# The tail rows of two batches stored by one transfer instead of two, and the last stores issued by SyncE alone

## Chip, cores and metric

One core of one Trainium2 chip runs the kernel. The metric is the device time of one execution in microseconds (us), lower is better. Three executions of the kernel before took 319.03, 319.62 and 318.98 us; the median is 319.03 us.

## The reference

A linear attention feeds a gated feed-forward layer. B = 8 batches of 576 tokens, 8 heads of 64 columns, so 4608 tokens of width 512; the hidden width is 1536. All is float32 at the borders.

```python
kv  = einsum('bhsd,bhse->bhde', k, v)
att = einsum('bhsd,bhde->bhse', q, kv)
att = att / sqrt(mean(att * att, -1) + 1e-6) * g_norm
x   = att.transpose(0, 2, 1, 3).reshape(4608, 512)
xn  = x / sqrt(mean(x * x, -1) + 1e-6) * rms_g
out = (silu(xn @ w_gate) * (xn @ w_val)) @ w_out      # (4608, 512) float32
```

## The kernel before

**Tokens.** Each batch has 576 tokens. The kernel takes the first 512 (`MAIN`) of each batch as one block, blocks 0 to 7. The last 64 (`TAIL`) of all eight batches make a ninth block, number 8, again 512 tokens. Block 8 is cut into four chunks of 128 tokens; chunk `c` holds the tail of batch `2c` in partitions 0 to 63 and that of batch `2c + 1` in partitions 64 to 127. In the output these two groups of 64 rows are each contiguous (64 rows of 2 KB), but they lie 576 rows apart.

**Stages of a block.** Class `Att` makes the normalised rows of a block. Class `Ffn` multiplies them: `up(j)` for the 12 slices of the hidden width (gate and value products of TensorE into two PSUM banks, SiLU on ScalarE, product on VectorE), then four times a down product of 128 tokens (12 matmuls into one PSUM bank), a copy of that bank to SBUF, and a store. The order is written out by hand: the loop over `n` runs `up` for 12 units and then a down product for 4 units, with the attention work of the next block hung between the units. In block 8 nothing is hung in any more.

**The down products of the last block.** For chunks 0, 1 and 2 of block 8, `down` runs 12 matmuls of 512 columns (L529), `down_out` copies the bank on ScalarE (L104, called from L537) and stores it from SyncE (L542). For chunk 3, `down_last` splits the 512 output columns into three parts of 256, 128 and 128 columns in three PSUM banks (L567). Two of them are copied by ScalarE (L104) and the last by VectorE (L106); the columns 0 to 255 are stored after the first copy, and the columns 256 to 511 after the third (L576).

**The buffers of the stores.** The tile `o_sb` is 128 partitions by two chunks by 512 columns of float32, and its pool has two buffers that are taken in turn. Chunks 0 and 1 of block 8 share one buffer, chunk 2 has the other, and `down_last` takes a new tile, which is the buffer of chunks 0 and 1 again. So the first copy of chunk 3 waits until the stores of chunks 0 and 1 have landed.

**Queues.** All loads and stores are issued by SyncE (queue q1 of the profile) but for three small groups issued by ScalarE (queue q10): two loads of `v` at the start, the two norm vectors (`gam`, L601 and L602), and one store of chunk 3. The program ends (L1069) when SyncE has seen the last store land.

Of the kernel before, what the change touches and what calls it, by code (L numbers as in the profile page):

```python
# [20 lines left out]
def kernel(  # L21
# [12 lines left out]
    nc = tc.nc  # L34

    B, H, S, D = q.shape
    d_model = H * D
# [5 lines left out]
    MAIN = 128 * T  # L43
    TAIL = S - MAIN
# [57 lines left out]
    def cast(engine, dst, src):  # L102
        if engine is SC:
            engine.copy(out=dst, in_=src)  # L104
        else:
            engine.tensor_copy(out=dst, in_=src)  # L106
# [161 lines left out]
    class Att:  # L268
        def __init__(self, n):
            self.n = n  # L270
            self.tail = n == B
            self.outa = {}
            self.xna = {}
            self.sq = {}
            self.qt = None
# [186 lines left out]

    class Ffn:
        def __init__(self, n):
            self.n = n
# [66 lines left out]
        def down_out(self, c, engine=None):  # L534
            if c % 2 == 0:
                self.o_sb = osb_pool.tile([128, 2, d_model], FP32, name="o_sb")
            cast(engine or SC, self.o_sb[:, c % 2, :], self.o_ps[c])  # L537
            n = self.n
            if n == B:
                for u in range(2):  # L540
                    r0 = (2 * c + u) * S + MAIN
                    nc.sync.dma_start(  # L542
                        out=out[r0 : r0 + TAIL, :], in_=self.o_sb[u * TAIL : (u + 1) * TAIL, c % 2, :]
                    )
            elif c % 2 == 1 and n == 0:
                r0 = 256 * (c // 2)
                rows = out[r0 : r0 + 256, :].rearrange("(p c t) d -> t p c d", c=2, t=2)
                for t in range(2):
                    nc.sync.dma_start(out=rows[t], in_=self.o_sb[64 * t : 64 * t + 64])
            elif c % 2 == 1:  # L550
                rows = out[n * S : n * S + MAIN, :].rearrange("(p t) d -> p t d", t=T)[:, c - 1 : c + 1, :]
                nc.sync.dma_start(out=rows, in_=self.o_sb)
# [5 lines left out]
        def down_last(self, c):  # L558

            o_sb = osb_pool.tile([128, 2, d_model], FP32, name="o_sb")[:, 0, :]  # L560
            parts = (
                (0, 256, ops_pool, "o_ps", SC), (256, 384, gps_pool, "g_ps", SC), (384, 512, vps_pool, "v_ps", DVE),
            )
            for lo, hi, p, nm, engine in parts:
                ps = p.tile([128, MAIN], FP32, name=nm)[:, 0 : hi - lo]
                for j in range(NF):
                    PE.matmul(  # L567
                        ps, lhsT=self.h[:, j, c * 128 : (c + 1) * 128], rhs=wo_sb[:, j, lo:hi],
                        start=(j == 0), stop=(j == NF - 1),
                    )  # L570
                cast(engine, o_sb[:, lo:hi], ps)
                for d0, done in ((0, 256), (256, 512)):
                    if hi == done:
                        for u in range(2):
                            r0 = (2 * c + u) * S + MAIN
                            (nc.sync if u or hi < d_model else nc.scalar).dma_start(  # L576
                                out=out[r0 : r0 + TAIL, d0:done], in_=o_sb[u * TAIL : (u + 1) * TAIL, d0:done]
                            )

# [15 lines left out]
    for j in (0, 1):  # L597
# [5 lines left out]
        out=gam[NS : NS + 1, :].rearrange("o (i d) -> o i d", i=2),  # L603
        in_=g_norm.rearrange("(o d) -> o d", o=1).unsqueeze(1).to_broadcast([1, 2, D]),
# [97 lines left out]
    for j in (0, 1):  # L702
# [29 lines left out]
        out=gsq, in0=gcol, scalar=1.0 / d_model, in1=gcol, op0=OP.mult, op1=OP.mult  # L732
# [257 lines left out]
    for n in range(1, B + 1):  # L990
# [12 lines left out]
        if n < B:  # L1003
# [5 lines left out]
            for i in range(2):  # L1009
                u = o0 + 2 * i  # L1010
# [9 lines left out]
        b = n + 2  # L1020
# [53 lines left out]
```

## Time and profile before

| | |
|---|---|
| median of three executions | 319.03 us |
| the profiled execution, its own time | 319.61 us |
| its span, first to last instruction | 317.6 us |
| mean granted TensorE clock | 0.998 |
| busy: TensorE matmul / VectorE / ScalarE | 308.5 / 181.3 / 175.6 us |
| stores of chunks 0 to 2 of block 8 (L542) | 6, of 128 KB each |
| stores of chunk 3 (L576) | 4, of 64 KB each |

The profiled execution took 319.61 us, of which 317.6 us lie between its first and last instruction and 2.0 us around them. Three other executions have their median 0.58 us below it. A busy TensorE says that matmuls were in flight, not that it ran at its peak. A busy share is a mean over the whole run: the change concerns the last 12 us alone, and what those wait for has to be read from that stretch.

### The profile page before, as it was taken

What the parts mean: (1) busy time and instruction counts of PE and PEld (TensorE: products, weight loads), DVE (VectorE), ACT (ScalarE), POOL (GpSimd) and SP (SyncE); (2) the same over time, 40 slices, a digit from 0 to 9 for tenths busy, and PEclk for the clock granted to TensorE, in tenths of its full rate; (3) what the DMA queues carried; (4) which work ended last, traced back from release to release, by engine and by line L of the source; (5) the groups of instructions that cost most, each with busy time, mean ns of one, the idle gap of its engine ahead of it and who ended that gap; (6) DMA issues with size and microseconds to landing.
All of it is one profiled execution on the core that took longest, in us unless ns stands there. A gap on an engine that the chain in (4) does not pass through costs nothing.

```text
span 317.6 us, 5996 instructions
## 1 busy us (share of the span) xinstructions
PE 308.5 (97%) x2334; PEld 150.3 (47%) x2371; DVE 181.3 (57%) x378; ACT 175.6 (55%) x323; POOL 21.5 (7%) x46
## 2 busy tenths in 40 slices
PE   7899999999999999999999999999999999999995
PEld 3575446444444444444444444444444444444443
DVE  3776768679339922893289327941795079504310
ACT  3577367485667465746683768376745374233321
POOL 1174351100000000000000000000000000000000
PEclk9999999999999999999999999999999999999999
DMA  7999999685369267904790489939002710230014
GB/s 266 358 385 388 375 375 333 145 275 215 90 180 344 86 138 187 369 9 108 189 378 22 98 172 207 354 66 181 22 0 60 140 66 3 57 141 3 0 33 100
DMA packets 60712, 54.95 MB, mean 173 GB/s; under 512 B 36232, under 2 KB 45708, under 8 KB 60684
## 3 DMA queue, kind: packets, MB, share of 16 engines
q1 hardware_dynamic: 60304, 53.92, 56.7%
q10 hardware_dynamic: 380, 0.66, 0.6%
q8 instruction: 18, 0.29, 0.4%
q14 instruction: 10, 0.08, 0.1%
HBM read 37.75 MB, written 9.44 MB: 149 GB/s over the span
## 4 chain that ended last, share of the span: by engine, by line
PE 90%; DMA 5%; SPq 1%; another core or an unknown queue 1%; issue 1%; POOL 1%; DVE 0%; ACT 0%
PE v_ps L477 28%; PE g_ps L477 28%; PE o_ps L529 26%; DMA st<-in_moe_w_val_dram 3%; DMA st<-in_q_dram 2%; PE att_ps L286 2%; PE v_ps L529 1%; PE g_ps L529 1%; DMA out_dram<-o_sb 1%; PE att_ps L326 1%; PE o_ps L494 1%; POOL wv_sb L191 1%; PE o_ps L326 0%; PE att_ps L262 0%
## 5 line engine op out<-in xcount | busy, mean ns | idle before, releaser
L483 DVE TENSOR_TENSOR h_sb<-silu,v_ps 128x512 bf16<-128x512 bf16 x104 | 71.1, 684 | 99.9 <-ACT silu L482 68.1
L477 PE MATMUL v_ps<-xnt,wv_sb 128*128 128x512 bf16 x409 | 106.2, 379 | 0.7
L477 PE MATMUL g_ps<-xnt,wg_sb 128*128 128x512 bf16 x398 | 104.6, 379 | 0.7
L482 ACT ACTIVATE silu<-g_ps 128x512 bf16<-128x512 f32 x104 | 62.1, 597 | 70.1 <-PE g_ps L477 58.4
L529 PE MATMUL o_ps<-wo_sb,h_sb 128*128 128x512 bf16 x386 | 86.8, 379 | 0.4
L477 PEld LDWEIGHTS <-wv_sb 128*128 128x128 bf16 x416 | 40.7, 98 | 49.1
L529 PEld LDWEIGHTS <-h_sb 128*128 128x128 bf16 x420 | 40.6, 98 | 47.6 <-issue 0.4
L477 PEld LDWEIGHTS <-wg_sb 128*128 128x128 bf16 x416 | 39.5, 98 | 46.4
L104 ACT COPY o_sb<-o_ps 128x512 f32<-128x512 f32 (+1 forms) x34 | 19.6, 581 | 40.2 <-PE o_ps L529 36.6
L373 DVE TENSOR_TENSOR xna<-outa,s1y 128x512 bf16<-128x512 bf16 x28 | 17.9, 685 | 0.0
L104 ACT CAST qb<-st 128x512 bf16<-128x512 f32 (+1 forms) x30 | 16.2, 603 | 3.0 <-DMA st<-in_q_dram 3.0
L104 ACT CAST vb<-st 128x576 bf16<-128x576 f32 x25 | 15.7, 673 | 3.4 <-DMA st<-in_v_dram 3.4
L356 DVE TENSOR_REDUCE ssq<-sq 128x16 f32<-128x1024 bf16 x14 | 17.1, 1220 | 0.5
L356 DVE TENSOR_REDUCE ssq<-sqt 128x16 f32<-128x1024 bf16 x14 | 17.1, 1220 | 0.5
L104 ACT CAST kb<-st 128x576 bf16<-128x576 f32 x20 | 12.5, 673 | 0.0
L341 ACT ACTIVATE sq<-att_ps 128x512 bf16<-128x512 f32 x14 | 7.6, 594 | 4.3 <-PE att_ps L326 3.6
L355 DVE TENSOR_TENSOR sq<-sq,gsq 128x512 bf16<-128x512 bf16 x14 | 5.9, 422 | 4.9 <-ACT sq L341 4.9
L629 PE MATMUL att_ps<-kv_all 128*128 128x512 bf16 (+1 forms) x21 | 7.5, 486 | 1.2 <-DVE sel L618 1.2
L106 DVE CAST kb<-st 128x576 bf16<-128x576 f32 x12 | 6.1, 527 | 3.6 <-DMA st<-in_k_dram 3.5
L106 POOL CAST wo_sb<-st 128x512 bf16<-128x512 f32 x12 | 7.3, 635 | 7.4 <-DMA st<-in_moe_w_out_dram 7.4
L341 ACT ACTIVATE sqt<-o_ps 128x512 bf16<-128x512 f32 x14 | 7.6, 597 | 0.0
L347 ACT CAST outa<-o_ps 128x512 bf16<-128x512 f32 x14 | 7.5, 591 | 0.0
(150 smaller groups left out, 181.5 us busy)
## 6 DMA issues: line engine op xcount, KB each, us to landing
st<-in_k_dram SPq DMA_DIRECT2D x7, 1152.0 KB, 10.5
st<-in_v_dram SPq DMA_DIRECT2D x7, 1152.0 KB, 12.6
out_dram<-o_sb SPq DMA_DIRECT2D x14, 512.0 KB, 3.1
st<-in_q_dram SPq DMA_DIRECT2D x6, 1024.0 KB, 7.2
st<-in_moe_w_out_dram SPq DMA_DIRECT2D x6, 512.0 KB, 10.4
st<-in_moe_w_gate_dram SPq DMA_DIRECT2D x4, 512.0 KB, 10.4
st<-in_moe_w_val_dram SPq DMA_DIRECT2D x4, 512.0 KB, 9.8
st<-in_k_dram SPq DMA_DIRECT2D x4, 288.0 KB, 4.0
```

The costliest lines, as they stand in the source:

```text
L104: engine.copy(out=dst, in_=src)
L106: engine.tensor_copy(out=dst, in_=src)
L286: PE.matmul(self.kv_ps[x][to, a, :], lhsT=kb[rows, 2 * a + x, c, :], rhs=vb[rows, 2 * a + x, c, :], start=(a == 0 and c == 0), stop=(a == ...
L341: SC.activation(out=self.in_place(self.sq[i][:, 0], g), in_=bank, func=ACT.Square)
L347: SC.copy(out=self.in_place(rows, g), in_=bank)
L356: DVE.reduce_sum(out=self.ssq[:, c], in_=sq, axis=AX.X)
L373: DVE.tensor_tensor(out=self.xna[c], in0=self.outa[c], in1=self.alpha[:, c, :].to_broadcast([128, H, D]), op=OP.mult)
L477: PE.matmul(ps, lhsT=wt[:, s, j * 128 : (j + 1) * 128], rhs=x[:, s, :], start=(s == 0), stop=(s == NS - 1),)
L482: SC.activation(out=silu, in_=g_ps, func=ACT.Silu)
L483: DVE.tensor_tensor(out=self.h[:, j, :], in0=silu, in1=v_ps, op=OP.mult)
L529: PE.matmul(self.o_ps[c], lhsT=self.h[:, j, c * 128 : (c + 1) * 128], rhs=wo_sb[:, j, :], start=(j == 0), stop=(j == NF - 1),)
L629: PE.matmul(ps[:, 0:w], lhsT=warm_sb[:, 0:128], rhs=warm_sb[:, 0:w], start=True, stop=True, skip_group_check=True)
```

## The change

The two stores of a chunk of block 8 (partitions 0 to 63 to one batch's rows, partitions 64 to 127 to the next batch's) become one. Its SBUF side is all 128 partitions; its DRAM side is a view of the output with three dimensions, 2 batches by 64 rows by 512 columns, the batches 576 rows apart. The stores of chunk 3 become two transfers of 2 by 64 by 256, both issued by SyncE, where one of the four was issued by ScalarE before. Ten transfers become five; the bytes are the same. No other instruction is added, removed or moved.

```diff
+    tail_rows = out.rearrange("(b s) d -> b s d", s=S)[:, MAIN:S, :]
...
         def down_out(self, c, engine=None):
...
             if n == B:
-                for u in range(2):
-                    r0 = (2 * c + u) * S + MAIN
-                    nc.sync.dma_start(
-                        out=out[r0 : r0 + TAIL, :], in_=self.o_sb[u * TAIL : (u + 1) * TAIL, c % 2, :]
-                    )
+                nc.sync.dma_start(out=tail_rows[2 * c : 2 * c + 2], in_=self.o_sb[:, c % 2, :])
...
         def down_last(self, c):
...
                 for d0, done in ((0, 256), (256, 512)):
                     if hi == done:
-                        for u in range(2):
-                            r0 = (2 * c + u) * S + MAIN
-                            (nc.sync if u or hi < d_model else nc.scalar).dma_start(
-                                out=out[r0 : r0 + TAIL, d0:done], in_=o_sb[u * TAIL : (u + 1) * TAIL, d0:done]
-                            )
+                        nc.sync.dma_start(out=tail_rows[2 * c : 2 * c + 2, :, d0:done], in_=o_sb[:, d0:done])
```

## The prediction

> **What bounds the kernel now.** I read the page first: span and engines, DMA queues, then the end of the chain, the instructions of the end, and single stretches of DMA.
>
> ```profile
> span 317.6 us, 5996 instructions
> PE 308.5 (97%) x2334; PEld 150.3 (47%) x2371; DVE 181.3 (57%) x378; ACT 175.6 (55%) x323; POOL 21.5 (7%) x46
> DMA packets 60712, 54.95 MB, mean 173 GB/s; under 512 B 36232, under 2 KB 45708, under 8 KB 60684
> q1 hardware_dynamic: 60304, 53.92, 56.7%
> q10 hardware_dynamic: 380, 0.66, 0.6%
> ```
>
> TensorE is busy throughout, so up to 313.8 us the kernel is bound by matmuls, and the change leaves those alone. What it touches is the end. The chain of waits there, and the timeline of the same stretch (start, duration, what):
>
> ```profile
> 311.22 0.59 ACT o_sb L104
> 311.82 0.02 issue
> 311.83 2.11 DMA out_dram<-o_sb
> 313.95 0.28 DVE o_sb L106
> ```
>
> ```profile
> 306.65 6.29 SPq L542 DMA_DIRECT2D out_dram<-o_sb  x6
> 312.58 0.37 ACT L104 COPY o_sb<-o_ps 128x256 f32<-128x256 f32 x1 [0.77 <-PE o_ps L567]
> 313.00 0.83 PE L567 MATMUL v_ps<-wo_sb,h_sb 128*128 128x128 bf16 x12
> 313.38 1.75 SPq L576 DMA_DIRECT2D out_dram<-o_sb  x3
> 313.93 0.29 DVE L106 COPY o_sb<-v_ps 128x128 f32<-128x128 f32 x1 [9.72 <-DMA out_dram<-o_sb]
> 314.31 0.56 ACTq L576 DMA_DIRECT2D out_dram<-o_sb  x1
> ```
>
> TensorE ends at 313.83 us, VectorE's copy at 314.22, the last issue starts at 314.60. In a finer stretch of the DMA view (313 to 318 us) the last packet is done at 316.25. From there to the end of the span it takes 1.35 us (receipt and closing). So the stores of chunks 0 to 2 are covered by TensorE, and only 3.8 us after the last matmul belong to stores. How fast one DMA engine works is read from a stretch that holds one 512 KB store alone (281 to 290 us):
>
> ```profile
> DMA packets 144, 0.52 MB, mean 58 GB/s; under 512 B 16, under 2 KB 16, under 8 KB 144
> q1 hardware_dynamic: 144, 0.52, 14.2%
> ```
>
> 14.2% of 16 engines over 9 us are 20.45 engine-us for 512 KB: 25.6 GB/s for each engine. The densest slices of the page (385 and 388 GB/s of loads, 16 engines) give 24.2. The packets are 128 rows and 16 of under 512 B: one small packet for each engine that takes part. That tells how many engines a transfer used. On q10 this can be counted:
>
> ```profile
> st<-in_v_dram ACTq DMA_DIRECT2D x2, 288.0 KB, 4.4
> out_dram<-o_sb ACTq DMA_DIRECT2D x1, 64.0 KB, 2.0
> gam<-in_moe_rms_g_dram ACTq DMA_DIRECT2D x1, 2.0 KB
> gam<-in_g_norm_dram ACTq DMA_DIRECT2D x1, 0.5 KB
> ```
>
> The queue has 380 packets. Two loads of 128 rows with 16 small packets each are 288, the store of 64 rows with 16 is 80, which leaves 12. The `gam` transfers have 4 and 2 rows: with 4 and 2 small packets they make 8 + 4 = 12; with 16 each they would make 38. So here a transfer of two rows ran on two engines.
>
> **What the Trainium skill says.** Page "DMA: Bandwidth & Descriptors", section "Why a DMA increments its semaphore by 16 and not by 1": a transfer issued by SyncE or ScalarE is spread over k engines, k being the largest number up to 16 that divides the slowest dimension (of size over 1) of both sides, as the instruction carries it; and the k engines are the lowest-numbered ones. The trace agrees for 128, 64, 4 and 2 rows, by the count above. It can't tell this rule from "as many engines as rows, at most 16", since no transfer here has few outer and many inner rows. The section "Rules for kernel authors" says that two transfers of disjoint halves of the partitions should be one of 128 partitions, which speaks for the change; it also says that an outermost dimension under 16 confines the whole transfer to so few engines, which speaks against it.
>
> **The change part by part.** In the list of instructions that the changed kernel issues, the destinations are carried as 2x64x512 and 2x64x256; the two batches, 576 rows apart, can't fold into one dimension. By the rule k = 2, the same two engines for all five stores. Everything else on the engines is in the same order.
>
> (1) *Issues.* Five fewer: on SyncE 3 x 0.58 us (median of L542) and one of L576 (0.53), on ScalarE one of 0.56. Those of chunks 0 to 2 lie beside TensorE and are worth nothing. On the path, the last issue can follow VectorE's copy at 314.3 instead of 314.6: 0.3 us less, if the data can go at once.
>
> (2) *Data.* Chunks 0, 1, 2 bring 128 KB to each of the two engines, the halves of chunk 3 bring 64 KB each: 512 KB (524,288 bytes) for each engine. The rate of a lone engine under such a store isn't in the trace. The store of 4 KB packets gave 25.6 GB/s (20.5 us); the best that the view shows anywhere is a slice of 438 GB/s in the first 4 us, 27.4 for each engine (19.1 us), which I take as the upper end. As the lower end I take 20 (26.2 us), my estimate for one chain of smaller packets that goes a fifth worse than 25.6. I choose 24, a little under the page's 24.2, since these packets are 192 of 2 KB and 128 of 1 KB on each engine: 524,288 / 24,000 = 21.8 us.
>
> (3) *When it starts and ends.* The store of chunk 0 is issued at 306.65; before, its first packet came at 307.9 (stretch 306 to 309.4 us). From then on the two engines are never empty, as 128 KB take 131,072 / 24,000 = 5.46 us and the next chunk is issued every 2.6 us: chunk 0 until 313.3, chunk 1 until 318.8, chunk 2 until 324.3.
>
> (4) *The wait that grows.* The first copy of chunk 3 (L104, ScalarE) needs the buffer of chunks 0 and 1. Before, it ran at 312.58, with those stores landed. Now it waits for chunk 1's, done at 318.8 and with some 0.4 us of receipt (316.25 to SyncE's release at 316.6) at 319.2: 6.6 us later. Behind it stand ScalarE's copy of `g_ps`, VectorE's copy of `v_ps` and both last issues of SyncE. These follow by about 319.7 and 320.4, their data at 1.2 us after. That is before 324.3, so the transfer of chunk 2 hides this wait whole and it adds nothing. TensorE has ended by then, and no bank is wanted again. Without that cover the wait would be worth up to 6.6 us, but then (16 engines) it wouldn't exist.
>
> (5) *The sum.* Last packet at 307.9 + 21.8 = 329.7; with the closing 1.35 the span is 331.1, that is 13.5 us over 317.6. The gain of (1) is lost in this. Against the profiled execution's own 319.61 that is 333.1; against the median of the runs shown (319.03), **332.5 us**. With the ends of (2), 19.1 and 26.2 us, it is 329.8 and 336.9.
>
> **The rivals.**
>
> *All 16 engines.* If the spread goes by the number of rows, or by the SBUF side's 128 partitions, a chunk goes at once over 16 engines. For it: every store of before did, and the count of packets allows it. Against it: the page's rule, told with the very case of a small outer dimension. It decides at the number of small packets: 16 per store and not 2. Then the gain of (1) is real: the last issue at 314.3 instead of 314.6, and 128 rows of 1 KB together instead of two waves, by the pattern of the 313 to 318 us stretch 0.1 to 0.2 us less. Some 0.45 us less: 318.6, the end that isn't slower. A difference of 0.2% (0.64 us) is about what a measurement of this kernel can tell from none, so this is mostly "same"; above it only if the data goes still faster.
>
> *Two engines, but far slower.* A 64-row store of before, stretch 306 to 309.4 us, spent 33.2% of 16 engines x 3.4 us = 18.1 engine-us on 256 KB, 14.5 GB/s, against 25.6 for the 128-partition store. If a lone engine on 64 partitions (or on contiguous rows of the output) also got only that, 524,288 / 14,500 = 36.2 us, and the last packet comes at 344.1: a span of 345.5, 347 us against the median. For it: the same rows, the same partitions. Against it: there 16 engines share these partitions, here one engine has them to itself; the total was 14.5 x 16 = 232 GB/s, far over what two engines need.
>
> *The wait of (4) in series.* If the engines ran empty because of it, its time would come on top. By the times of (3) there are 3 us to spare, so I give it no chance of its own.
>
> **How the numbers follow.** Two engines at 20 to 27.4 GB/s: 0.82, with 332.5 us. Two engines far slower: 0.08. 16 engines: 0.10, of which 0.07 fall within 0.2% and 0.03 are faster by more. The range 329.8 to 337.0 is that of the first case and leaves out the other two, 0.18. Chances: faster 0.03, same 0.07, slower 0.90.
>
> **What would show it.** Two engines: packets under 512 B fall by 160 - 10 = 150 to 36082, and q10 keeps 300. From 314 to 330 us the DMA share is 2/16, about 0.12, with about 48 GB/s. Issue to landing grows from 2.3 us to about 7, 10 and 13 us for chunks 0, 1 and 2 (each waits for those before it), then 8 to 10. ScalarE's copy of chunk 3 starts near 319 us, with a store as the releaser, and SyncE's last wait is about 9 us where it was 1.4. With 80 fewer small packets (160 to 80), landings near 2.3 us and an end near 317 us, the prediction is wrong in its first step; with the share of 0.12 but an end elsewhere, in the rate of (2).

## The result and the profile after

The changed kernel takes 333.26 us (median of five, 332.62 to 333.96) where the kernel before takes 319.19 us (five, 318.98 to 319.96): 4.3% slower, ratio 1.0434 with an interval of 1.0414 to 1.0455. The forecast was 332.5 us, range 329.8 to 337.0. The profiled execution took 333.6 us with a span of 331.6.

The same lines of the page as before the change, and the last slices of DMA (40 slices of 8.3 us; the last three are the end):

```profile
span 331.6 us, 5988 instructions
PE 308.9 (93%) x2334; PEld 150.2 (45%) x2371; DVE 180.8 (55%) x378; ACT 175.6 (53%) x323; POOL 21.6 (7%) x46
DMA  7999998692677369347913898480045004100111
GB/s 273 359 385 387 375 374 261 171 345 73 157 218 277 61 170 336 107 63 187 359 59 73 186 208 330 101 154 2 0 127 128 1 2 127 63 3 0 35 52 41
DMA packets 60562, 54.95 MB, mean 166 GB/s; under 512 B 36082, under 2 KB 45558, under 8 KB 60534
q1 hardware_dynamic: 60234, 53.98, 54.0%
q10 hardware_dynamic: 300, 0.59, 0.5%
```

The work of the engines is the same to 0.5 us; the span is 14.0 us longer. The packets under 512 B fell from 36232 to 36082: 160 for ten stores became 10 for five, two for each. The end runs at about 50 GB/s and a share of 0.1. The timeline of the end (start, duration, what; the last bracket is idle time and what ended it), and who waited for whom there:

```profile
306.80 5.69 SPq L542 DMA_DIRECT2D out_dram<-o_sb  x3
313.14 0.83 PE L565 MATMUL v_ps<-wo_sb,h_sb 128*128 128x128 bf16 x12
320.09 0.37 ACT L104 COPY o_sb<-o_ps 128x256 f32<-128x256 f32 x1 [8.13 <-DMA out_dram<-o_sb]
320.26 0.29 DVE L106 COPY o_sb<-v_ps 128x128 f32<-128x128 f32 x1 [15.90 <-DMA out_dram<-o_sb]
320.49 1.48 SPq L572 DMA_DIRECT2D out_dram<-o_sb  x2
```

```profile
SPq L1063 <- DMA out_dram<-o_sb: 8.5, 2, 5.9
SPq L572 <- ACT o_sb L104: 8.1, 1, 8.1
```

TensorE ends at 313.97 us, as before (313.83). From there to the end of the span it is 17.6 us, where it was 3.8. I use this length, "the end after the last matmul", for all kernels below, since the last matmul itself ends anywhere from 313.1 to 315.0 us in the profiled executions.

The steady rate of the two engines is read from a stretch of the DMA view, 314.5 to 319.6 us, and their start from 308 to 314.5:

```profile
DMA packets 130, 0.26 MB, mean 51 GB/s; under 512 B 2, under 2 KB 2, under 8 KB 130
q1 hardware_dynamic: 130, 0.26, 13.2%
```

```profile
GB/s 25 50 0 25 25 50 25 25 50 25 0 25 50 25 0 25 50 50 50 25 50 50 50 50 50 50 50 50 50 50 50 50 50 50 50 50 50 50 50 50
DMA packets 128, 0.26 MB, mean 40 GB/s; under 512 B 0, under 2 KB 0, under 8 KB 128
```

One whole chunk (128 packets of 2 KB, two small ones) takes 5.1 us: 262,144 bytes / 5.1 us / 2 = 25.7 GB/s for each engine. The share of 13.2% of 16 engines is 2.1 engines at work. The first chunk takes 6.4 us: in its first 2.6 us the slices often hold nothing or one engine's packets. The view counts a packet in the slice in which it starts, and here the packets took longer: 12.8% of 16 engines over 6.5 us are 104 ns for each of 128 packets, 13.2% over 5.1 us are 84 ns.

### The profile page after: what moved, and what is told of

The parts are those of the page before. It is cut to its first block, busy times and chain, and to the rows that moved or that the text cites. A ratio compares the mean times of both kernels' runs of the same rounds, so it can differ in the third digit from the quotient of the medians.

```text
span 331.6 us, 5988 instructions
## 1 busy us (share of the span) xinstructions
PE 308.9 (93%) x2334; PEld 150.2 (45%) x2371; DVE 180.8 (55%) x378; ACT 175.6 (53%) x323; POOL 21.6 (7%) x46
## 2 busy tenths in 40 slices
DMA packets 60562, 54.95 MB, mean 166 GB/s; under 512 B 36082, under 2 KB 45558, under 8 KB 60534
## 4 chain that ended last, share of the span: by engine, by line
PE 86%; DMA 8%; SPq 1%; issue 1%; POOL 1%; ACT 0%; DVE 0%; ACTq 0%
PE v_ps L479 27%; PE g_ps L479 27%; PE o_ps L531 25%; DMA out_dram<-o_sb 3%; DMA st<-in_moe_w_val_dram 3%; DMA st<-in_q_dram 2%; PE att_ps L286 1%; PE v_ps L531 1%; PE g_ps L531 1%; PE att_ps L326 1%; PE o_ps L496 1%; POOL wv_sb L191 1%; PE o_ps L326 0%; PE att_ps L262 0%; SPq L589 0%
```

## Experiments

Two theories. **Theory:** the outermost dimension of the DRAM side, 2, confines each store to two engines, and the bytes per engine set the end. **Rival:** merging as such costs, or three dimensions, or the one issuing queue. Times are beside runs of the kernel before on the same chip (319.06 to 319.75 us, by the set of runs), so the ratio is the measure.

**Same merged store, outermost dimension 4, 8 and 64.** The bytes, the number of transfers and their issuer stay; the assignment of rows to chunks changes, by the order in which VectorE's product writes the columns of block 8.

```diff
 # outermost 4 (outer4)
-out=tail_rows[2 * c : 2 * c + 2]
+out=tail_rows[4 * (c // 2) : 4 * (c // 2) + 4, 32 * (c % 2) : 32 * (c % 2) + 32]
 # outermost 8 (outer8)
+out=tail_rows[:, 16 * c : 16 * c + 16]
 # outermost 64 (outer16)
+out=tail_rows[2 * c : 2 * c + 2].rearrange("u r d -> r u d")
 # in Ffn.up, for block 8 (here for outer16; the others alike)
+to = self.h[:, j, :].rearrange("p (c r u) -> p c u r", c=4, u=2)
+a, b = (t.rearrange("p (c u r) -> p c u r", c=4, u=2) for t in (silu, v_ps))
+DVE.tensor_tensor(out=to, in0=a, in1=b, op=OP.mult)
```

> Chunk c of block 8 holds 32 rows of each of four batches, so its one store has the destination 4x32x512 (chunk 3: twice 4x32x256); number of transfers, bytes, issuer and waits are those of the changed kernel, and VectorE's product writes the columns in the new order, in two instructions for each slice. Theory (the outermost dimension sets the number of engines, and bytes per engine set the end): 4 engines, 20 packets under 512 B for the five stores, 256 KB per engine, 10.4 us of packets at the 80 ns (2 KB) and 42 ns (1 KB) that the changed kernel showed; chunks 0 to 2 nearly keep pace with TensorE; end near 321 us of span, 322 us of time (321.4 to 322.8). Rival (a merged store of 128 partitions, or three dimensions, or SyncE alone is what costs): no change against the changed kernel, 333 us.

> As the run with four batches, but a chunk holds 16 rows of each of the eight batches: destination 8x16x512. Theory: 8 engines, 40 small packets, 1.3 us for a chunk, so the engines wait for TensorE; the end comes from the last issue, 319.2 us (318.7 to 319.8), as before the change. Rival: 333 us.

> A chunk holds the same two tails as in the changed kernel, but its partitions alternate between the two batches (partition 2r+u is row r of batch 2c+u), so the same store is carried as 64x2x512: outermost dimension 64 and not 2, all else as in the changed kernel; VectorE's product writes single columns 2 apart. Theory: 16 engines, 80 small packets for the five stores, end 0.3 to 0.5 us ahead of the kernel before, 318.7 us, provided that the product with the changed order stays under the 1.7 us that TensorE leaves it for a slice. Rival (merged store as such): 333 us.

| outermost dimension | small packets of the last stores | time | ratio to before | end after the last matmul |
|---|---|---|---|---|
| 2 (the changed kernel) | 10 | 333.26 us | 1.0434 (1.0414 to 1.0455) | 17.6 us (331.6 - 313.97) |
| 4 | 20 | 325.99 us | 1.0197 (1.0174 to 1.0219) | 10.2 us (324.1 - 313.85) |
| 8 | 40 | 320.89 us | 1.0039 (1.0024 to 1.0053) | 5.1 us (319.3 - 314.25) |
| 64 | 80 | 319.71 us | 1.0007 (0.9995 to 1.0018) | 3.9 us (318.8 - 314.95) |

The brackets have the span and the end of the last matmul. The last matmuls of the kernels with 4, 8 and 64:

```profile
313.02 0.83 PE L571 MATMUL v_ps<-wo_sb,h_sb 128*128 128x128 bf16 x12
313.42 0.83 PE L569 MATMUL v_ps<-wo_sb,h_sb 128*128 128x128 bf16 x12
314.12 0.83 PE L569 MATMUL v_ps<-wo_sb,h_sb 128*128 128x128 bf16 x12
```

The DMA view's packet counts over the stores alone, in the same order, and the rate with 64 (307 to 318.8 us, slices of 0.3 us):

```profile
DMA packets 661, 1.06 MB, mean 59 GB/s; under 512 B 20, under 2 KB 276, under 8 KB 660
```

```profile
DMA packets 681, 1.06 MB, mean 81 GB/s; under 512 B 40, under 2 KB 296, under 8 KB 680
```

```profile
GB/s 0 0 0 0 0 0 0 361 368 160 0 0 0 0 0 125 375 368 21 0 0 0 0 0 278 403 208 0 288 156 0 28 0 90 326 28 0 0 0 0
DMA packets 721, 1.06 MB, mean 90 GB/s; under 512 B 80, under 2 KB 336, under 8 KB 720
```

Five stores with 4, 8 and 16 small packets each: the number of engines follows the outermost dimension, up to 16. The merged store as such costs nothing that can be measured (64x2x512: 1.0007). That is the theory's main point, and the rival (333 us in each) falls. No product of VectorE in the run with 64x2x512 took over 0.74 us (L489, 675 to 733 ns, all blocks; 672 to 690 in the changed kernel), so the new order doesn't disturb. But the sizes were missed: with 4 and 8 I expected 322 and 319.2 us, and the gain of 0.3 to 0.5 us that 64 was to bring did not come. The first is taken up below, the second under step (1).

**One half of the change alone.**

```diff
 # only_main: chunk 3 as in the kernel before, chunks 0 to 2 merged
+nc.sync.dma_start(out=tail_rows[2 * c : 2 * c + 2], in_=self.o_sb[:, c % 2, :])
 # only_last: chunks 0 to 2 as before, the two halves of chunk 3 merged
+nc.sync.dma_start(out=tail_rows[2 * c : 2 * c + 2, :, d0:done], in_=o_sb[:, d0:done])
 # sync_only: the kernel before, nothing merged
-(nc.sync if u or hi < d_model else nc.scalar).dma_start(
+nc.sync.dma_start(
```

> Only the stores of chunks 0 to 2 are merged; chunk 3 is stored by four transfers as before (one from ScalarE). Theory: engines 0 and 1 are busy with chunks 0 to 2 until 324.8 us, then take their sixteenth of the four last stores, 0.7 us; with 1.4 us of closing the span is about 326.9, the time 328.5 us (327.8 to 329.2). Rival (only what is issued last counts, as the earlier stores lie beside TensorE): 319.2 us.

> Only the stores of chunk 3 are merged (2x64x256 each, both from SyncE); chunks 0 to 2 are stored by six transfers as before. Theory: two engines move 128 KB each in packets of 1 KB, 5.4 us from about 314.7 us on, and up to 1.3 us more for the stalls that the changed kernel shows in its first packets; span 321.5 to 322.8, time 323.5 us (322.8 to 324.5). Rival (chunk 3 is not what costs): 319.2 us.

> The kernel before with the one store that ScalarE issued moved to SyncE: ten transfers of 64 rows, nothing merged. Theory: the two stores after VectorE's copy are issued one after the other, the last starts about 0.5 us later, 319.6 us (319.1 to 320.0). Rival (SyncE alone is what costs): several us more.

Measured: 328.86 us (ratio 1.0284, 1.0255 to 1.0312), 323.80 us (1.0139, 1.0108 to 1.0170) and 319.95 us (1.0021, 1.0010 to 1.0032), all within what was expected. Chunks 0 to 2 were covered by TensorE before the change and still bring the larger part, 9.8 us, when they are confined to two engines; chunk 3 brings 4.7 us. Issuing all ten from SyncE costs little: 0.9 us by the medians, 0.7 by the ratio, and 0.6 in the profiled executions, whose ends after the last matmul are 4.4 and 3.8 us.

**Two issuing queues on the same two engines.**

```diff
-nc.sync.dma_start(out=tail_rows[2 * c : 2 * c + 2], in_=self.o_sb[:, c % 2, :])
+(nc.scalar if c == 1 else nc.sync).dma_start(out=tail_rows[2 * c : 2 * c + 2], in_=self.o_sb[:, c % 2, :])
-nc.sync.dma_start(out=tail_rows[2 * c : 2 * c + 2, :, d0:done], in_=o_sb[:, d0:done])
+(nc.sync if hi < d_model else nc.scalar).dma_start(out=tail_rows[2 * c : 2 * c + 2, :, d0:done], in_=o_sb[:, d0:done])
```

> The changed kernel with the stores of chunk 1 and of the second half of chunk 3 issued by ScalarE instead of SyncE. Theory (two DMA engines are the limit, whoever issues): 333.2 us (332.4 to 334), q10 gains 128 + 2 + 128 + 2 packets. Rival (one issuing queue is the limit, since all last stores went to SyncE): half of the 14 us comes back, about 326 us.

335.71 us (1.0508, 1.0482 to 1.0534): the rival's 326 is out, but the time is 2.4 us over the changed kernel and not equal to it. Its timeline and a stretch of its DMA (324.5 to 333 us, 40 slices):

```profile
309.73 0.60 ACTq L542 DMA_DIRECT2D out_dram<-o_sb  x1
312.31 0.55 SPq L542 DMA_DIRECT2D out_dram<-o_sb  x1
324.29 0.37 ACT L104 COPY o_sb<-o_ps 128x256 f32<-128x256 f32 x1 [12.01 <-DMA out_dram<-o_sb]
324.69 0.51 SPq L572 DMA_DIRECT2D out_dram<-o_sb  x1
```

```profile
GB/s 48 58 19 0 0 0 24 14 39 39 29 34 43 10 39 34 48 48 24 5 14 29 48 48 48 48 48 48 48 48 48 48 48 48 48 48 48 39 0 0
```

Chunk 1 (from ScalarE) and chunk 2 (from SyncE) now share the engines (by their small packets they are done at 323.8 and 325.1 us, where in the changed kernel it was 319.6 and 324.8), so chunk 1's store lands late, and the first copy of chunk 3 starts at 324.29 where it started at 320.09. The engines run empty at 325.1, for about 0.7 us (the zeros), and then start slowly again (slices of 5 to 48 until 329). This is the wait of the prediction's step (4) without its cover. By an estimate from these slices the gap costs 0.7 us and the slow start 1.3 (3.4 us at 30 GB/s instead of 48), 2.0 of the 2.4 us.

**The wait itself.**

```diff
-osb_pool = pool("osb", 2)
+osb_pool = pool("osb", 3)
```

> The changed kernel with three o_sb buffers instead of two, so that ScalarE's first copy of chunk 3 no longer waits for the stores of chunks 0 and 1. Theory (the wait is hidden by the two engines' backlog): the copy runs near 312.7 us again and the end stays, 333.2 us (332.6 to 334). Rival (the wait stands in series with the stores): 6 us less, 327 us.

333.70 us (1.0440, 1.0421 to 1.0459), the end after the last matmul 17.5 us: nothing gained. The copy runs early, as expected, and the time moves into the issue:

```profile
313.08 0.37 ACT L104 COPY o_sb<-o_ps 128x256 f32<-128x256 f32 x1 [0.72 <-PE o_ps L565]
```

```profile
313.48 6.87 SPq L572 DMA_DIRECT2D out_dram<-o_sb  x2
```

So in the changed kernel the longest wait of the end, 8.1 us of ScalarE and SyncE, costs nothing: the two engines are full meanwhile.

**Why 4 and 8 engines were slower than worked out.** In the stretch 308.4 to 313.4 us of the kernel with 8 (40 slices of 0.125 us, two stores):

```profile
DMA  4577431442355554541044944334343455535220
GB/s 115 98 66 49 33 33 16 49 49 66 131 197 197 197 197 180 197 164 49 16 115 66 98 33 33 33 33 66 66 98 131 180 213 180 229 131 197 115 82 0
q1 hardware_dynamic: 272, 0.52, 43.0%
```

Each store begins with about 1.2 us at 16 to 115 GB/s and then runs mostly at 180 to 229, around the 205 of 8 times 25.6. A store of 1.3 us becomes one of 2.5. The engines are not empty in the slow slices, as shares of mostly 0.3 to 0.7 show; they take longer for each packet: 43.0% of 16 engines over 5 us are 134 ns for each of 256 packets of 2 KB. With 4 engines the stretch 307.9 to 312.9 us runs at a mean of 56 GB/s, where 4 times 25.6 would be 102. One explanation was that engines that read partitions 32 apart share a port of SBUF, as the port table named in the next expectation has it: with four batches in a chunk, engines 0 and 1 would read partitions 0 to 31 and 32 to 63 in step. A run with two engines on just these partitions tells:

```diff
 # outer4's chunks, each stored by two transfers of 64 partitions (chunk 3's halves alike)
+for u in range(2):
+    b = 4 * (c // 2) + 2 * u
+    rows = tail_rows[b : b + 2, 32 * (c % 2) : 32 * (c % 2) + 32]
+    nc.sync.dma_start(out=rows, in_=self.o_sb[u * TAIL : (u + 1) * TAIL, c % 2, :])
```

> The chunks of the run with four batches (32 rows of each), but stored by two transfers of 2x32x512 (2x32x256) each, one for partitions 0 to 63 and one for 64 to 127: again two engines, again 512 KB for each, but now the two engines read partitions 0 to 31 and 32 to 63 (then 64 to 95 and 96 to 127) at the same time. Theory A (only the number of engines and the bytes per engine count): 333.5 us (332.5 to 335). Theory B (engines that read partitions 32 apart share a port of SBUF, as the port table of the Trainium skill's page SBUF — State Buffer, section Door 1: The DMA port swizzle, has it, which is why the run with four batches came out at 326 and not 322 us): packets slower than 84 ns, as the 113 ns (2 KB, mean) of the run with four batches; 341 to 350 us.

334.00 us (1.0450, 1.0429 to 1.0472), as by theory A. In its stretch 311.8 to 321.8 us it has nearly the same rate as the changed kernel (49 and 51 GB/s):

```profile
DMA packets 243, 0.49 MB, mean 49 GB/s; under 512 B 6, under 2 KB 6, under 8 KB 242
```

The two engines ran nearly in step there: by the small packets they ended the stores of this stretch 0.02 to 0.10 us apart, about one packet of 84 ns at most. If the rows are divided as the expectation takes it, shared ports cost two engines nothing that shows, and theory B falls in this form. What remains is what the stretches show: stores on 2, 4 or 8 engines often go slowly for a time when they find the engines idle (6.4 us for the first chunk of the changed kernel, 5.1 for the next; again after the gap in the run with two queues). With 8 engines each chunk finds them idle and pays anew, in the changed kernel only the first chunk pays. But this isn't the whole of it, as stores issued long before are slow too. The issues of chunks 1 and 2 with 4 engines, and its rate from 306 to 324 us (40 slices of 0.45 us):

```profile
309.26 3.13 SPq L548 DMA_DIRECT2D out_dram<-o_sb  x2
GB/s 0 0 0 0 32 23 14 23 64 68 100 100 73 46 59 55 59 59 77 91 64 109 68 73 96 100 100 91 89 100 96 93 80 66 84 73 25 0 0 0
```

Chunk 1 was issued at 309.3, and the four engines ended chunk 0 between 311.8 and 312.8; still the rate is 46 to 59 GB/s from 311.9 to 314.1. The run with the shared ports has such a stretch too (26 to 29 GB/s from 320.8 to 322 us, with a store of chunk 2 still queued). Why stores on few engines go slowly at these times isn't settled.

**Is there a version that beats the kernel before?** The store of 64x2x512 removes five transfers at no cost, so I moved its last issue back to ScalarE.

```diff
 # on top of outer16
-nc.sync.dma_start(out=tail_rows[2 * c : 2 * c + 2, :, d0:done]...
+(nc.sync if hi < d_model else nc.scalar).dma_start(out=tail_rows[2 * c : 2 * c + 2, :, d0:done]...
```

> The run with 64x2x512 with the last store (columns 256 to 511 of chunk 3) issued by ScalarE instead of SyncE. In that run SyncE began this issue 0.40 us after VectorE's copy had ended; before the change ScalarE began its own 0.09 us after it. Theory: 0.3 us less than the run with 64x2x512, the last packet about 2.1 us after the last matmul where it was 2.4 before the change; 318.8 us beside 319.1 before (a ratio of 0.998 to 1.001). Rival (the order of the product on VectorE or the single transfer costs as much elsewhere): no better than before.

319.59 us beside 319.50 (1.0003, 0.9992 to 1.0014), the end after the last matmul 3.8 us as before the change: no difference that can be measured. The last packet ended 2.3 us after the last matmul, where 2.1 was expected and 2.4 was measured before the change. The lines of its last copy and issue:

```profile
314.38 0.29 DVE L106 COPY o_sb<-v_ps 128x128 f32<-128x128 f32 x1 [9.68 <-PE v_ps L569]
314.75 0.69 ACTq L576 DMA_DIRECT2D out_dram<-o_sb  x1
```

The issue starts 0.08 us after the copy, as expected, but takes 0.69 us where the one of 64 rows took 0.56.

## Why the prediction was right, step by step

**Two engines.** Right, and the counts are exact: 36082 small packets and 300 packets on q10. The trace of the kernel before couldn't tell "outermost dimension" from "number of rows"; the series 2, 4, 8, 64 at 128 rows each does. It agrees with the Trainium skill's page "DMA: Bandwidth & Descriptors", section "Why a DMA increments its semaphore by 16 and not by 1". Of the two rules of its section "Rules for kernel authors" that pulled in opposite directions, the one on the outermost dimension decides here. On 16 engines the merged store of a chunk does move faster, in 0.8 us (the three slices of 361, 368 and 160 GB/s) where its two stores of 64 rows took 1.4 us before; but this lies beside TensorE, and the kernel's time does not change measurably.

**Step (2), the rate.** 24 GB/s was taken. From the first packet at 308.1 to the last at 330.2 the two engines moved 524,288 bytes each in 22.1 us, 23.7 GB/s. The value is near, but its make-up was not foreseen. Chunk 0 took 6.4 us with its slow start, chunks 1 and 2 took 5.1 each (a steady 25.7 GB/s by elapsed time, close to the 25.6 of the 512 KB store), and the two halves of chunk 3 together 5.4 (24 GB/s, in packets of 1 KB), where 5.46 was forecast for each of the four. That the slow start of 1.3 us was nearly made up by the faster chunks is luck. The upper end of the rate was misread: the view of the first 4 us has a slice of 461 GB/s, not 438 at most. That is 28.8 for each engine and would put the range's lower end at 328.9 us; the result lies inside either way. For 4 and 8 engines, where the start is paid with more stores, the same way of working it out was 4 us and over 1 us short.

**Steps (3) and (4).** The last packet was expected at 329.7 and came at 330.2; the closing took 1.4 us, as expected. The first copy of chunk 3 was expected at 319.2 and started at 320.09: the first packet came 0.2 us later, chunk 0 took 1.0 us more than forecast and chunk 1 took 0.3 less. SyncE's last waits, expected at 9 us, are 8.5 in two pieces. That the wait is hidden was right, and shown by the third buffer. That there were 3 us to spare held for the order of issue in the changed kernel; with two queues it was used up.

**Step (1), the issues.** The gain of 0.3 us for 16 engines was wrong in size. In the kernel with 64x2x512 the end is 3.9 us and not 3.3 to 3.5. Its lines:

```profile
314.09 2.18 SPq L576 DMA_DIRECT2D out_dram<-o_sb  x2
315.04 0.29 DVE L106 COPY o_sb<-v_ps 128x128 f32<-128x128 f32 x1 [9.67 <-PE v_ps L569]
```

VectorE's copy ends at 315.33. SyncE's second issue ends at 316.27 and takes 0.54, so it starts at 315.73, 0.40 us after the copy. The last issue from SyncE before the change also came 0.38 us after the copy (314.22 to 314.60), which I had put down to SyncE being busy; in the kernel with 64x2x512 SyncE's own issue before it had ended at 314.63, so that isn't the reason there. In the forecast this had no weight, as the gain was lost in the 13.5 us anyway.

**The rivals.** Sixteen engines and the far slower engine both failed: 2 small packets for each store, and 25.7 GB/s where the second rival had 14.5.

## What to carry to other kernels

Before two transfers are merged, look at the dimensions that the merged one carries: its outermost dimension set how many DMA engines it got (2, 4, 8 and 16 for 2, 4, 8 and 64), and a 2 there turned 1 MB of mostly hidden stores into 14 us. Where the rows could be reordered so that the long dimension was outermost, the same merged transfer cost nothing measurable. A long wait at the end isn't by itself a cost: ask whether the DMA engines that set the end are idle during it.

## What was not expected of the hardware

- Stores on 2, 4 or 8 engines went slowly at times, most often when they found the engines idle: for 2.6 us with two engines and 1.2 us with 8, which cost 1.3 and 1.2 us. The engines were at work on packets that took longer (134 ns on average with 8, where 84 is the steady time). Stores of 128 rows on 16 engines didn't show it (361 GB/s in the first slice with 64x2x512). The cause is open.
- An issue can be held while earlier stores are queued: in the run with three buffers the two issues of SyncE took 3.43 and 3.01 us, where the same issues took 0.51 and 0.52 in the changed kernel. At the first of them none of the three chunks before it had landed on the two engines.
- The DMA view gives no time from issue to landing for the last stores on 2 engines. By their small packets they ended 7.7, 10.2 and 12.8 us after their issues for chunks 0 to 2 and 7.0 and 8.8 us for chunk 3, where the prediction had about 7, 10 and 13, then 8 to 10.
